# One more matrix product of 64 columns ahead of each step of a gated two-layer network (Trainium2, one core)

## The chip, the cores and the metric

The kernel runs on one core of one Trainium2 chip. The metric is the device time of one execution in microseconds (us); of several executions the median is taken. Each kernel also has one execution that the hardware profiler recorded, with its own time and its span (first to last instruction).

## The reference

Attention with a capped score for 4 x 12 heads of 448 tokens and 64 features, then two matrix layers over all 1792 tokens with a gate between them.

```python
scores = cap * np.tanh((scale * np.matmul(q, k.transpose(0, 1, 3, 2))) / cap)
scores = scores - np.max(scores, axis=-1, keepdims=True)
attn = np.exp(scores)
attn = attn / (np.sum(attn, axis=-1, keepdims=True) + 1e-09)
out = np.matmul(attn, v)            # (4, 12, 448, 64)
x = out.transpose(0, 2, 1, 3).reshape(4 * 448, 768)
h = x @ w_in                        # w_in: 768 x 2048
g = h * np.cos(h)
return g @ w_out                    # w_out: 2048 x 768
```

## The kernel before, in words

The first part is attention. A table of due times sets the order of its pieces; its products are of type float32. It leaves x, transposed, as two tiles `xh` and `xl` (a high part rounded to the type float32r, and the rest), each 128 partitions x 6 chunks of features x 1792 tokens.

The second part is the two layers. The 2048 hidden features are 16 blocks of 128, taken in 8 groups of two (`GF` = 2), and the 1792 tokens are 4 batches of 448 (`S`). A step is one group with one batch, so there are 32 steps. In each, two `Unit`s (j = 0 and 1, one for each hidden block) compute the first layer's product with `hidden`: 6 chunks times 3 terms (high x high, low x high, high x low) are 18 matmuls of a 128 x 128 weight tile with 448 columns, summed in one PSUM bank. A bank holds 512 columns of float32, so its columns 448 to 511 stay unused. Then the `Block` of the step before computes the second layer's product: three calls, each of 24 / 2 = 12 matmuls for two output chunks. So PE gets 36 matmuls of the first layer (L196) and 36 of the second (L601) in a step, 72 in all, all float32r with 448 columns.

Units use the pool tag `single`, which has two banks, so that unit 0 of a step gets the bank that unit 0 of the step before had. The second layer's sums go to the tags `pair` and `rest`. Behind the product of a unit, ScalarE and VectorE compute the gate from the bank: `turns` (L558), `whole_turns`, `reduce` (L566, L567), `cosine` (L570), `gate` (L573, the last reader of the bank), `high` (L576) and `low` (L579). VectorE also adds the second layer's sums into `acc` (L613) and turns the weights, which arrive as 64-bit words, into float32r pairs (L246 to L256).

`terms` changes the order of the three terms from group to group: even groups begin with the high part of x, odd groups with the low part; both begin with the high part of the weights (`wh`).

The first step's units are computed earlier, inside the last stretch of attention: `begin(0)` and `begin(1)` put their products into banks of the tag `pair`.

Of the kernel before, what the change touches and what calls it, by code (L numbers as in the profile page):

```python
# [19 lines left out]
B, H, S, D = 4, 12, 448, 64  # L20
# [149 lines left out]
class Banks:  # L170
# [14 lines left out]
    def product(self, i):  # L185

        return self.rest() if i == 2 else self.pair()


def hidden(nc, wts, f, xh, xl, h, b):  # L190
    hi, lo = wts.get("wi", f)
    toks = slice(S * b, S * b + S)
    for k in range(KC):
        ks = slice(128 * k, 128 * k + 128)
        for i, (w, x) in enumerate(terms(f // GF, hi, lo, xh, xl)):
            nc.tensor.matmul(h[:, 0:S], lhsT=w[:, ks], rhs=x[:, k, toks],  # L196
                             start=(k == 0 and i == 0), stop=(k == KC - 1 and i == 2))


def terms(G, wh, wl, xh, xl):  # L200

    if G % 2:
        return (wh, xl), (wh, xh), (wl, xh)
    return (wh, xh), (wl, xh), (wh, xl)
# [334 lines left out]
class Unit:  # L539
# [6 lines left out]
    def product(self, bank=None):  # L546
        if self.h is None:
            h = bank if bank is not None else self.m.banks.single()
            hidden(self.m.nc, self.m.wts, self.f, self.m.xh, self.m.xl, h, self.b)
            self.h = h[:, 0:S]  # L550

# [218 lines left out]
```

## Time and profile before

| what | value |
|---|---|
| median of 3 runs | 664.13 us (663.76 to 664.15) |
| profiled execution, its time | 664.33 us |
| profiled execution, its span | 662.5 us |
| mean granted TensorE clock | 0.994 of full |
| PE (matmuls) busy | 651.9 us, 98% |
| PEld (weight loads) busy | 490.0 us, 74% |
| DVE (VectorE) busy | 493.8 us, 75% |
| ACT (ScalarE) busy | 318.1 us, 48% |

The busy time of an engine is the time in which at least one of its instructions was under way. Matmuls overlap in the records, so the busy time of PE is not a sum of their durations; the distance from start to start tells their pace. The time of the profiled execution is 1.8 us more than its span.

### The profile page before, as it was taken

Reading aid. Unit: us, or ns where it says so; the run is one execution under the profiler, and the core shown is the slowest. Engines: PE = TensorE matmul, PEld = TensorE weight load, DVE = VectorE, ACT = ScalarE, POOL = GpSimd, SP = SyncE. Lnnn points to the kernel's source line nnn. Section 1 sums busy time; section 2 is a strip of 40 time slices with the busy share of each in tenths; the row PEclk is TensorE's granted clock in tenths of the full one; section 3 lists DMA queues with packets and bytes.
Section 4 is the critical chain, followed back from the end, with each engine's and each line's share of the span. In section 5 each row is a group of like instructions: output and inputs, shape, how many; then the busy total and the mean of one; then the engine's idle time right before and its main releaser. Section 6 shows DMA issues by size and latency. Waiting matters only on the chain.

```text
span 662.5 us, 8791 instructions
## 1 busy us (share of the span) xinstructions
PE 651.9 (98%) x3563; PEld 490.0 (74%) x3563; DVE 493.8 (75%) x739; ACT 318.1 (48%) x385; POOL 62.0 (9%) x39
## 2 busy tenths in 40 slices
PE   7999999999999999999999999999999999999996
PEld 2333333333489999999999999999999999999995
DVE  1599999997778876677777776677777776677663
ACT  4999999999724433333333333333333333333220
POOL 0001011000011111111111111111111121111000
PEclk9899999999999999999999999999999999999998
DMA  7044332542001211111112111111112111110224
GB/s 257 10 151 147 111 139 92 182 150 102 1 1 50 94 49 47 48 47 48 48 52 85 55 47 48 48 48 49 48 57 72 63 48 48 48 48 0 84 85 171
DMA packets 19616, 49.41 MB, mean 75 GB/s; under 512 B 2160, under 2 KB 5232, under 8 KB 19568
## 3 DMA queue, kind: packets, MB, share of 16 engines
q1 hardware_dynamic: 19568, 48.77, 21.8%
q8 instruction: 30, 0.49, 0.3%
q14 instruction: 18, 0.15, 0.1%
HBM read 43.25 MB, written 5.51 MB: 74 GB/s over the span
## 4 chain that ended last, share of the span: by engine, by line
PE 98%; ACT 1%; DMA 0%; issue 0%; DVE 0%
PE single L196 35%; PE pair L601 24%; PE rest L601 12%; PE single L421 12%; PE pair L328 9%; PE rest L337 3%; PE rest L430 2%; PE pair L196 1%; DMA capt<-in_cap_dram 0%; PE rest L102 0%; ACT t L362 0%; ACT late L347 0%; ACT t L347 0%; DVE acc L613 0%; ACT cabs L126 0%
## 5 line engine op out<-in xcount | busy, mean ns | idle before, releaser
L570 ACT ACTIVATE y<-y,angles 128x448 f32<-128x448 f32 x64 | 43.0, 672 | 149.4 <-DVE y L567 149.4
L558 ACT ACTIVATE v<-single,angles 128x448 f32<-128x448 f32 x62 | 39.2, 633 | 101.4 <-PE single L196 101.4
L246 DVE TENSOR_SCALAR u<-u 128x768 f32<-128x768 f32 x28 | 15.7, 561 | 94.9 <-ACT u L231 94.9
L613 DVE TENSOR_TENSOR acc<-pair,acc 128x896 f32<-128x896 f32 x56 | 60.6, 1083 | 3.9 <-PE pair L601 3.9
L576 ACT CAST gh<-y 128x448 fp32r<-128x448 f32 x64 | 36.3, 567 | 49.6 <-DVE y L573 49.6
L328 PE MATMUL pair<-qk 64*128 64x448 f32 x264 | 58.6, 562 | 0.0
L328 PEld LDWEIGHTS pair<-qk 64*128 64x128 f32 x264 | 22.7, 186 | 36.2 <-issue 20.1
L347 ACT ACTIVATE t<-pair,inv 128x896 f32<-128x896 f32 x48 | 45.9, 1004 | 6.0 <-PE pair L328 5.5
L579 DVE TENSOR_TENSOR gl<-y,gh 128x448 fp32r<-128x448 f32 x64 | 40.8, 638 | 4.0 <-ACT gh L576 4.0
L362 ACT ACTIVATE t<-t,capt 128x1792 f32<-128x1792 f32 x24 | 42.8, 1783 | 0.4
L401 DVE TENSOR_TENSOR sum<-t 128x896 f32<-128x896 f32 x24 | 26.1, 1088 | 21.9 <-ACT t L362 21.9
L567 DVE SCALAR_TENSOR_TENSOR y<-v,y 128x448 f32<-128x448 f32 x64 | 40.0, 625 | 2.2
L421 PE MATMUL single<-late,v 128*32 128x448 f32 x368 | 40.7, 542 | 0.0
L573 DVE TENSOR_TENSOR y<-single,y 128x448 f32<-128x448 f32 x62 | 38.2, 616 | 2.7 <-ACT y L570 2.7
L566 DVE SCALAR_TENSOR_TENSOR y<-v,single 128x448 f32<-128x448 f32 x62 | 38.5, 621 | 2.1
L421 PE MATMUL single<-t,v 128*32 128x448 f32 x368 | 39.4, 547 | 0.0
L601 PE MATMUL pair<-gh,wo0h 128*128 128x448 f32 x96 | 35.3, 368 | 0.0
L601 PE MATMUL pair<-gh,wo0l 128*128 128x448 f32 x96 | 35.3, 368 | 0.0
L601 PE MATMUL pair<-gl,wo0h 128*128 128x448 f32 x96 | 35.3, 368 | 0.0
L196 PE MATMUL single<-xl,wi2h 128*128 128x448 f32 x96 | 35.3, 368 | 0.0
L196 PE MATMUL single<-xh,wi2h 128*128 128x448 f32 x96 | 35.3, 368 | 0.0
L196 PE MATMUL single<-xh,wi2l 128*128 128x448 f32 x96 | 35.3, 368 | 0.0
(143 smaller groups left out, 1609.5 us busy)
## 6 DMA issues: line engine op xcount, KB each, us to landing
w<-in_w_in_dram SPq DMA_DIRECT2D x32, 384.0 KB, 3.6
w<-in_w_out_dram SPq DMA_DIRECT2D x32, 384.0 KB, 3.6
qk<-in_qkv_dram SPq DMA_DIRECT2D x22, 480.0 KB, 5.5
v<-in_qkv_dram SPq DMA_DIRECT2D x23, 256.0 KB, 4.0
out_dram<-acc SPq DMA_DIRECT2D x11, 448.0 KB, 2.5
w<-in_qkv_dram SPq DMA_DIRECT2D x2, 240.0 KB, 3.8
second<-in_qkv_dram SPq DMA_DIRECT2D x1, 480.0 KB, 5.7
out_dram<-acc SPq DMA_DIRECT2D x2, 224.0 KB, 2.8
```

The lines of the kernel that those rows point to most:

```text
L196: nc.tensor.matmul(h[:, 0:S], lhsT=w[:, ks], rhs=x[:, k, toks], start=(k == 0 and i == 0), stop=(k == KC - 1 and i == 2))
L328: self.nc.tensor.matmul(ps[:, h, 0:S], lhsT=x[mine, 128 * g:128 * g + 128], rhs=x[mine, Q], start=True, stop=True)
L347: self.nc.scalar.activation(out, ps[:, :, 0:S], AF.Tanh, scale=self.inv)
L362: self.nc.scalar.activation(t, t, AF.Exp, scale=self.capt)
L421: self.nc.tensor.matmul(self.acc[q][e][o], lhsT=self.v[q, a][:, g, d], rhs=t, start=(g == first), stop=(g == last), tile_position=(0, o.st ...
L558: m.nc.scalar.activation(self.v, self.h, AF.Identity, bias=m.quarter, scale=1.0 / (2.0 * math.pi))
L566: m.nc.vector.scalar_tensor_tensor(self.y, self.v, -TWO_PI_HI, self.h, op0=ALU.mult, op1=ALU.add)
L567: m.nc.vector.scalar_tensor_tensor(self.y, self.v, -TWO_PI_LO, self.y, op0=ALU.mult, op1=ALU.add)
L570: self.m.nc.scalar.activation(self.y, self.y, AF.Sin, bias=self.m.half_pi)
L579: self.m.nc.vector.tensor_sub(self.g[1][:, self.j], self.y, self.g[0][:, self.j])
L601: m.nc.tensor.matmul(y[:, e, 0:S], lhsT=w[:, c], rhs=x[:, j], start=(j == 0 and k == 0), stop=(j == GF - 1 and k == 2))
L613: m.nc.vector.tensor_add(acc, y[:, e, 0:S], acc)
```

## The change

Before the product of unit 0 of each step, one more matmul is issued. It multiplies the weight tile of chunk 0 (high part) with the first 64 tokens of chunk 0 of `xh`, and writes 64 columns into columns 448 to 511 of the unit's bank. Nothing reads them. It happens once in each of the 32 steps, the first of them in `begin(0)`.

```diff
     def product(self, bank=None):
         if self.h is None:
             h = bank if bank is not None else self.m.banks.single()
+            if self.j == 0:
+                hi, x = self.m.wts.get("wi", self.f)[0], self.m.xh
+                self.m.nc.tensor.matmul(h[:, S:512], lhsT=hi[:, 0:128], rhs=x[:, 0, 0:512 - S], start=True, stop=True)
             hidden(self.m.nc, self.m.wts, self.f, self.m.xh, self.m.xl, h, self.b)
             self.h = h[:, 0:S]
```

PE's instructions before, where one step of the layers ends and the next begins (`rest` is the bank of the last sum of the second layer, `single` the bank of unit 0; `wi0h` and `wi0l` are the high and low part of a weight tile; the semaphores that an instruction waits for stand in brackets):

```order
L601 MATMUL rest<-gh,wo1h 128x448
L601 MATMUL rest<-gh,wo1l 128x448
L601 MATMUL rest<-gl,wo1h 128x448
L196 MATMUL single<-xh,wi0h 128x448 [waits DVE_49]
L196 MATMUL single<-xh,wi0l 128x448
L196 MATMUL single<-xl,wi0h 128x448
```

The same place of PE in the changed kernel (three lines further down in the source, so L601 is L604 there):

```order
L604 MATMUL rest<-gh,wo1h 128x448
L604 MATMUL rest<-gh,wo1l 128x448
L604 MATMUL rest<-gl,wo1h 128x448
L551 MATMUL single<-xh,wi0h 128x64 [waits DVE_49,PE_49]
L196 MATMUL single<-xh,wi0h 128x448
L196 MATMUL single<-xh,wi0l 128x448
L196 MATMUL single<-xl,wi0h 128x448
```

The new matmul takes over the wait for VectorE, and a wait for PE's own semaphore is added: the columns 448 to 511 of this bank were last written by the new matmul of the step before, and its end is what is waited for, 73 matmuls back. For the second wait a separate waiting instruction stands ahead of the new matmul in 30 of the 32 steps (not shown above). The kernel before has 23 such waiting instructions in its layers, one of them ahead of the second layer's first matmul of the step that begins at 217 us. On the other engines the order is the same as before.

The beginning of the first unit, inside attention, before (PE; `t_1342` is a tile of exponentials, `pair` the bank of the unit):

```order
L421 MATMUL single<-t_1302,v 32x448 x2
L421 MATMUL single<-t_1342,v 32x448 x2
L196 MATMUL pair<-xh,wi0h 128x448 [waits Activation_49]
L196 MATMUL pair<-xh,wi0l 128x448 [waits Pool_49]
L196 MATMUL pair<-xl,wi0h 128x448
```

The same place in the changed kernel:

```order
L421 MATMUL single<-t_1302,v 32x448 x2
L421 MATMUL single<-t_1342,v 32x448 x2
L551 MATMUL pair<-xh,wi0h 128x64 [waits Activation_49]
L196 MATMUL pair<-xh,wi0h 128x448
L196 MATMUL pair<-xh,wi0l 128x448 [waits Pool_49]
L196 MATMUL pair<-xl,wi0h 128x448
```

Here too the new matmul takes over the wait of the first one of the unit, and nothing else moves.

## Rows read from the trace of the kernel before

**Rows 1.** The page: span, and the ended-last chain's shares by engine and line.

```profile
span 662.5 us, 8791 instructions
...
PE 98%; ACT 1%; DMA 0%; issue 0%; DVE 0%
PE single L196 35%; PE pair L601 24%; PE rest L601 12%; PE single L421 12%; PE pair L328 9%; PE rest L337 3%; PE rest L430 2%; PE pair L196 1%; DMA capt<-in_cap_dram 0%; PE rest L102 0%; ACT t L362 0%; ACT late L347 0%; ACT t L347 0%; DVE acc L613 0%; ACT cabs L126 0%
```

**Rows 2.** The chain in order of time, 379.89 to 412 us: start, length, what.

```profile
380.71 7.44 PE single L196 x36
388.15 4.96 PE pair L601 x24
393.12 2.48 PE rest L601 x12
395.60 7.44 PE single L196 x36
```

**Rows 3.** All waits of PE in the execution: total us, times, longest us.

```profile
PE pair L328 <- ACT t L347: 2.0, 1, 2.0
PE idle L102 <- DVE busy L112: 1.2, 1, 1.2
PE rest L102 <- ACT cabs L126: 1.0, 1, 1.0
```

**Rows 4.** Stretches: length, each engine's busy us (instructions), granted clock, DMA.

```profile
175.00:187.20 12.20, 12.20 (x85) 8.07 (x78) 10.21 (x17) 4.35 (x6) 0.00 (x0) 1.00 0.00 0
395.60:410.48 14.88, 14.88 (x73) 13.51 (x73) 11.09 (x19) 5.18 (x9) 1.85 (x1) 1.00 0.18 54
187.20:648.00 460.80, 460.80 (x2232) 418.48 (x2231) 340.64 (x521) 158.59 (x247) 53.55 (x29) 1.00 0.16 54
```

**Rows 5.** PE's timeline where a step ends and the next begins: start, length.

```profile
409.90 0.37 PE L601 MATMUL rest<-gh,wo1h 128*128 128x448 f32 x1
410.11 0.37 PE L601 MATMUL rest<-gh,wo1l 128*128 128x448 f32 x1
410.31 0.37 PE L196 MATMUL single<-xh,wi0h 128*128 128x448 f32 x1
410.52 0.37 PE L196 MATMUL single<-xh,wi0l 128*128 128x448 f32 x1
```

**Rows 6.** The weight loads of the same place.

```profile
410.11 0.19 PEld L196 LDWEIGHTS single<-xh,wi0h 128*128 128x128 f32 x1
410.32 0.19 PEld L196 LDWEIGHTS single<-xh,wi0l 128*128 128x128 f32 x1
```

**Rows 7.** Weight loads and matmuls of `begin(0)`, timelines of PEld and PE.

```profile
175.56 0.19 PEld L196 LDWEIGHTS pair<-xh,wi0h 128*128 128x128 f32 x1 [0.73 <-ACT late L347]
175.67 0.19 PEld L196 LDWEIGHTS pair<-xh,wi0l 128*128 128x128 f32 x1
175.87 0.19 PEld L196 LDWEIGHTS pair<-xl,wi0h 128*128 128x128 f32 x1
...
175.56 0.47 PE L196 MATMUL pair<-xh,wi0h 128*128 128x448 f32 x1
175.87 0.36 PE L196 MATMUL pair<-xh,wi0l 128*128 128x448 f32 x1
...
179.11 0.36 PE L196 MATMUL pair<-xl,wi0h 128*128 128x448 f32 x1
```

**Rows 8.** Weight loads of an odd group, two in a row of one tile.

```profile
400.19 0.19 PEld L196 LDWEIGHTS single<-xl,wi3h 128*128 128x128 f32 x1
400.40 0.19 PEld L196 LDWEIGHTS single<-xh,wi3h 128*128 128x128 f32 x1
400.60 0.19 PEld L196 LDWEIGHTS single<-xh,wi3l 128*128 128x128 f32 x1
```

**Rows 9.** VectorE's timeline: a unit's gate and the step's first own work.

```profile
404.36 0.62 DVE L573 TENSOR_TENSOR y<-single,y 128x448 f32<-128x448 f32 x1
...
410.97 1.08 DVE L613 TENSOR_TENSOR acc<-rest,acc 128x896 f32<-128x896 f32 x1
415.68 0.56 DVE L246 TENSOR_SCALAR u<-u 128x768 f32<-128x768 f32 x1 [3.63 <-ACT u L231]
```

**Rows 10.** PE's timeline at the change from the first layer to the second, one step.

```profile
224.11 0.37 PE L196 MATMUL single<-xl,wi1h 128*128 128x448 f32 x1
224.31 0.37 PE L601 MATMUL pair<-gh,wo0h 128*128 128x448 f32 x1
224.52 0.37 PE L601 MATMUL pair<-gh,wo0l 128*128 128x448 f32 x1
```

## The prediction

> **What bounds the kernel now.** I read the page first: the chain that ended last is 98% PE, and its largest parts are the two layers' matmuls, L196 and L601 [rows 1]. The chain in order of time then shows how the layers are laid out: 36 matmuls of the first layer in 7.44 us, 24 and 12 of the second in 4.96 and 2.48 us, and the next step begins at once [rows 2]. So a step is 14.88 us for 72 matmuls, 0.2067 us each, and the reader is to see that the chain never leaves PE there. The waits of PE say the same from the other side: in the whole execution it waited for another engine three times, 4.2 us together, all of them lines of attention or of the start (L102, L328) and none in the layers [rows 3]. The stretches give the other engines' share of one step: VectorE works 11.1 of 14.88 us, ScalarE 5.2, GpSimd 1.9, the DMA engines 18% [rows 4]. The granted clock is 1.00 through all the layers and in the stretch of the two early units, which is the 2.4 GHz level [rows 4]. Whatever PE does longer in a step therefore moves the end by as much, unless it fits into a gap of PE, and no such gap shows: the product that begins a step starts 0.20 us behind the last one of the step before [rows 5].
>
> **How a matmul and its weight load follow each other.** Each matmul has a weight load of its own. In the steady pace the load for a matmul starts as the matmul ahead of it starts, and not earlier: the load for the product of 410.31 starts at 410.11, the one for 410.52 at 410.32 [rows 5, 6]. So one weight tile is loaded ahead and no more. A record of a load is 0.19 us long, a pace is 0.21 us, and one could read from this that the load sets the pace. The beginning of the early units says that it doesn't. There the first load had nothing to hide behind: it starts at 175.56, and the second load starts at 175.67, 0.11 us later, while the second matmul starts at 175.87, 0.20 us behind that [rows 7]. Since a load starts as the matmul ahead starts, the first matmul began to stream at 175.67. So the weights are in place 0.11 us after the load begins, though its record is longer, and a matmul of 448 columns holds the array for some 0.20 us, behind which a load of 0.11 us is hidden.
>
> **The change, part by part.** It removes nothing. It adds 32 matmuls of 64 columns, 32 weight loads, 30 waiting instructions, and no work elsewhere.
>
> The new matmul's own load hides behind the last matmul of the step before, as the load at 410.11 does now [rows 6]: 0.11 us under 0.2067 us, nothing. If that cover were gone, it would cost its 0.11 us again.
>
> The new matmul itself streams 64 columns. No product of this width is in the trace. Scaled from 448 columns it is 64 / 448 x 0.2067 = 0.03 us; with what the pace of 0.2067 us holds beyond 448 columns at 2.4 GHz (0.187 us), 0.02 us, as a fixed part, it is 0.027 + 0.02 = 0.047 us.
>
> What comes behind it is the point. The load for the first real product can start only as the new matmul starts, and needs 0.11 us. The real product cannot begin before that, however short the new one is. Until now its load lay under a matmul of 0.2067 us; now it lies under one of 0.03 to 0.05 us and sticks out. So a step becomes longer by the load, 0.11 us, in which the 64 columns are hidden, and not by the columns. That the weights are the same tile doesn't help as far as the trace goes: in odd groups two matmuls in a row use the high part of one tile, and it is loaded twice, 0.21 and 0.20 us apart as everywhere [rows 8].
>
> The price has two ends. Below it is the columns alone, 0.03 us, if this one load could come earlier; above it is a full place in the pace, 0.207 us, if a load and its matmul could not follow each other faster than everywhere in the layers. I take 0.11 us, since the one place that shows a load without cover has it. If the 0.02 us came on top, it would be 0.13 us.
>
> On this the Trainium skill speaks, and against the load as the price: "TensorE: Matmul & The Clock Gate", section "Back-to-back issue gap", lists an isolated product of 1 to 64 columns at a floor of about 25 ns, or about 62 ns where the sequencer's microcode decodes it. By that table the sum would be an estimated 0.8 to 2.0 us. By the uncovered load of [rows 7] it is 3.5 us. The table leaves the weight load out, and I go by the row.
>
> The waiting instructions cost nothing, I say. VectorE's last read of a bank, its gate, starts at 404.36 and takes 0.62 us, and the bank is next written at 410.31, over 5 us later [rows 5, 9]. The wait for PE's own semaphore is for a matmul of a step ago, 14.9 us. That a separate waiting instruction on PE by itself costs no time is seen at 224.31, where the kernel before has one: the distances are 0.20 and 0.21 us, the common pace [rows 10]. The matmuls ahead are still streaming while PE takes in the wait; without that cover its price has, from these rows, no more than their rounding, 0.01 us, which is 0.3 us in 30 steps.
>
> The other engines get 0.11 us more in each step. VectorE, the busiest, waits in each step anyway: it ends its last addition of one step at 412.05 and starts the next weight work at 415.68 [rows 9]. Nothing of theirs becomes late. The one new matmul inside attention, at `begin(0)`, meets a PE that is busy throughout 175 to 187 us [rows 4], so it counts like the rest.
>
> The sum: 32 x 0.11 = 3.5 us. The profiled execution has 664.33 us, so 667.8 us by its own time; it lies 0.2 us above the median of the runs, so against 664.13 us the forecast is 667.6 us. That is 0.5%, and I call 0.2%, 1.3 us, about what a measurement here tells from no change.
>
> **The rivals.**
> The pace of the load: a load and a matmul together need 0.207 us, always. For it speaks that a load's record is 0.19 us and that loads stand 0.207 us apart throughout the layers [rows 6, 8]; against it that the second load of the early unit started 0.11 us behind the first [rows 7]. It gives 32 x 0.207 = 6.6 us, 670.7 us.
>
> The columns alone: the load comes early enough after all, or is left out for the same tile. Then 32 x 0.03 to 0.047 = 1.0 to 1.5 us, 665.1 to 665.6 us, at the edge of no change. Against it stand [rows 6, 8].
>
> No cost at all, since PE would have waited at a step's beginning: 664.1 us. Against it stand [rows 3, 5].
>
> Not slower, but faster: the pace is not a constant. In the first early unit, 16 distances from 175.87 to 179.11 are 3.24 us, 0.2025 us each [rows 7], against 0.2067 us in the layers [rows 2]. What makes the difference the trace doesn't show; that unit came behind an uncovered load. If a short product, with its uncovered load, brought the shorter pace back for the rest of the step, it would give 72 x 0.0042 = 0.30 us and cost 0.11 us: 0.19 us gained in each of 31 steps, 6 us, 658 us. It decides from 26 products per step at the shorter pace on (0.11 / 0.0042). Against it: the pieces of the chain have 0.2067 us per product throughout, also behind the begin of a step [rows 2].
>
> **How the numbers follow.** The uncovered load, at 0.10 to 0.13 us, has 72%: 667.3 to 668.3 us, with the scatter of the runs 667.0 to 668.7 us. The full place has 12% (670.7 us), the columns alone 7% (half of it under 0.2%), no cost 4%, the faster pace 5%. The range has to take in the full place to hold 8 in 10: 666.7 to 670.9 us, 84%. Slower by over 0.2%: 72 + 12 + 4 = 88%; within 0.2%: 7%; faster: 5%.
>
> **What would show it.** In the profile after, the load for the first real product of a step should start with the new matmul, and this product some 0.11 us behind it; a step should be 14.99 us instead of 14.88 us, with PE's waits unchanged, the granted clock in the layers still 1.00, and the distances between the other products still 0.2067 us. A real product 0.03 to 0.05 us behind the new one would prove the columns right, 0.2 us the full place. I am wrong as a whole if the distances of the 72 others change, or if PE waits at the new matmul.

## The result, and the profile after

The changed kernel takes 657.96 us (median of 4 runs, 656.83 to 658.62) against 664.14 us before (4 runs, 663.76 to 664.27): a ratio of 0.9906, 95% interval [0.9889, 0.9923]. It is faster by 6.2 us, where 667.6 us and a range of 666.7 to 670.9 us had been forecast. The rival that ends on the other side, a shorter pace of the other products, had been given 5% and 658 us.

The page after, its span and the granted clock in 40 slices, which answer to [rows 1] and to the clock of [rows 4]:

```profile
span 655.7 us, 8917 instructions
...
PEclk9999999999999999999999999999999999999999
```

PE still is 98% of the chain, and its waits are the three of [rows 3] to 0.1 us, so no wait went away. A step of the layers after, as a stretch (length, busy us of PE, PEld, DVE, ACT, POOL with instructions, granted clock, DMA), which answer to [rows 4]:

```profile
405.58:420.28 14.70, 14.70 (x74) 13.63 (x73) 11.08 (x18) 5.16 (x9) 1.85 (x1) 1.00 0.17 54
```

A step is 14.70 us, where it was 14.88 us with one product less, at the same granted clock of 1.00. PE's timeline at the begin of such a step, and at its end, which answers to [rows 5] (L604 is the second layer here, L551 the new product):

```profile
405.38 0.36 PE L604 MATMUL rest<-gh,wo1l 128*128 128x448 f32 x1
405.58 0.19 PE L551 MATMUL single<-xh,wi0h 128*128 128x64 f32 x1
405.61 0.45 PE L196 MATMUL single<-xh,wi0h 128*128 128x448 f32 x1
405.90 0.36 PE L196 MATMUL single<-xh,wi0l 128*128 128x448 f32 x1
...
420.08 0.36 PE L604 MATMUL rest<-gh,wo1l 128*128 128x448 f32 x1
420.28 0.19 PE L551 MATMUL single<-xh,wi0h 128*128 128x64 f32 x1
```

And the weight loads at its begin, which answer to [rows 6]:

```profile
405.38 0.19 PEld L551 LDWEIGHTS single<-xh,wi0h 128*128 128x128 f32 x1
405.59 0.19 PEld L196 LDWEIGHTS single<-xh,wi0h 128*128 128x128 f32 x1
405.69 0.19 PEld L196 LDWEIGHTS single<-xh,wi0l 128*128 128x128 f32 x1
405.90 0.19 PEld L196 LDWEIGHTS single<-xl,wi0h 128*128 128x128 f32 x1
```

Two things are to be seen. The first real product's load starts with the new product, at 405.59, and the load behind it at 405.69. Since a load starts as the matmul ahead starts, the real product starts 0.11 us behind the new one (405.58 to 405.69). That is the price that had been forecast. (The record of the real product starts at 405.61 already and is 0.45 us long where others have 0.36 us; it seems to take in the wait for its weights.) But from 405.90 to 420.08 there are 70 distances in 14.18 us, 0.2026 us each, where all were 0.2067 us before. This is the pace of the early unit in [rows 7], now in the layers from step 1 on. The two early units themselves, the first of them with the new product ahead of it, ran at 0.2067 us in this profile.

From the first real or new product of step 1 to the last product the profiles have 468.5 us before (187.11 to 655.63) and 462.8 us after (185.06 to 647.88), 5.7 us less. Worked out: 2268 products at 0.0040 us less are 9.1 us, 31 new products at 0.11 us are 3.4 us, together 5.7 us less. The rest of the 6.8 us between the two spans lies ahead of the layers and behind them. `begin(0)` starts at 175.56 us in the profile before and at 173.33 us after, and in the thirteen profiles of this study anywhere from 173.2 to 176.0 us, whatever the kernel. The kernel before itself took 661.4 to 664.7 us on the chips of the later runs. With such a scatter, a median that meets a forecast to 0.1 us, as some do below, does so in part by luck; the distances in the profiles are the better evidence.

### The profile page after: what moved, and what is told of

Read it like the earlier page. It is cut to its first block, busy times and chain, and to the rows that moved or that the text cites. A ratio compares the mean times of both kernels' runs of the same rounds, so it can differ in the third digit from the quotient of the medians.

```text
span 655.7 us, 8917 instructions
## 1 busy us (share of the span) xinstructions
PE 644.2 (98%) x3595; PEld 493.5 (75%) x3595; DVE 493.7 (75%) x739; ACT 317.9 (48%) x385; POOL 61.9 (9%) x39
## 4 chain that ended last, share of the span: by engine, by line
PE 98%; ACT 1%; DMA 0%; issue 0%; DVE 0%
PE single L196 35%; PE pair L604 24%; PE rest L604 12%; PE single L421 12%; PE pair L328 9%; PE rest L337 3%; PE rest L430 2%; PE pair L196 1%; DMA capt<-in_cap_dram 0%; ACT t L362 0%; PE rest L102 0%; ACT late L347 0%; PE single L551 0%; ACT t L347 0%; DVE acc L616 0%
## 5 line engine op out<-in xcount | busy, mean ns | idle before, releaser
L196 PE MATMUL single<-xl,wi3h 128*128 128x448 f32 x96 | 35.1, 366 | 0.0
L604 PE MATMUL pair<-gh,wo0l 128*128 128x448 f32 x96 | 35.1, 365 | 0.0
L604 PE MATMUL pair<-gh,wo0h 128*128 128x448 f32 x96 | 35.1, 365 | 0.0
L196 PE MATMUL single<-xh,wi3l 128*128 128x448 f32 x96 | 35.1, 365 | 0.0
```

Source lines behind the costliest of these rows:

```text
L604: m.nc.tensor.matmul(y[:, e, 0:S], lhsT=w[:, c], rhs=x[:, j], start=(j == 0 and k == 0), stop=(j == GF - 1 and k == 2))
```

## The experiments

The theory after the result: PE has two paces for these products, and keeps either until something disturbs the rhythm of load and product; the new product (called a push from here on) disturbs it, and the short pace comes of that. Rivals: that the push is needed in each step, that it is the waiting instructions, or that any added instruction does it.

**One push, ahead of step 1.**

```diff
-            if self.j == 0:
+            if (self.f, self.b) == (0, 1):
```

> The new product once, ahead of unit 0 of step 1, and nowhere else. Theory (the pace has two states, and the new product's uncovered load moves PE from 0.2067 to 0.2027 us per product, where it stays): 31 steps and the last block are 2268 products, each 0.004 us shorter, 9.1 us less for 0.1 us more: 655.2 us, with 0.2027 us from step 1 to the end. Rival A (each step needs its own push, the short pace dies out within a step): 0.2 us less at most, 663.9 us. Rival B (it is the 30 separate waiting instructions or the semaphore counts, none of which stands here): 664.2 us.

Ten runs with a median of 661.87 us, in two groups: three of 654.52 to 655.47 us (the short group), seven of 661.44 to 664.63 us (the long group, where the kernel before lay too, with 661.41 to 664.55 us). Neither the theory nor a rival had said that. The profiled execution was one of the short group; its chain in order of time (start, length, what):

```profile
187.18 7.37 PE single L196 x36
194.55 4.87 PE pair L604 x24
199.42 2.43 PE rest L604 x12
201.85 7.30 PE single L196 x36
209.15 4.86 PE pair L604 x24
```

From the push on all is short: 7.30 us for 36 products are 0.2028 us each, and it stays so to the end, 30 steps without another push. So A and B fall for this execution: one push is enough, with no waiting instruction ahead of it. What happened in the seven others was open.

**One push, ahead of the first early unit.** The same line with `(0, 0)`.

> The new product only ahead of the first early unit, inside attention. Theory: what counts is the state in which the layers begin, and the attention products behind the first early unit start it anew, so the layers run at 0.2067 us: 664.1 to 664.3 us. Rival (any one such product sets the short pace for good): 655 us.

655.30 us (653.43 to 656.14, 4 runs), ratio 0.9875 [0.9846, 0.9905]: the time of the rival. But its reason isn't the rival's. In the profile, which shows one of the four runs, the first early unit runs at the short pace and the second at the long one. So the layers begin at the long pace, and change in the middle of step 1, far from any push. PE's timeline there:

```profile
195.90 0.37 PE L604 MATMUL pair<-gh,wo1l 128*128 128x448 f32 x1
196.10 0.36 PE L604 MATMUL pair<-gl,wo1h 128*128 128x448 f32 x1
196.30 0.36 PE L604 MATMUL pair<-gh,wo0h 128*128 128x448 f32 x1
196.50 0.36 PE L604 MATMUL pair<-gh,wo0l 128*128 128x448 f32 x1
196.69 0.37 PE L604 MATMUL pair<-gl,wo0h 128*128 128x448 f32 x1
```

And the weight loads, with VectorE's work ahead of them:

```profile
195.28 0.62 DVE L582 TENSOR_TENSOR gl<-y,gh 128x448 fp32r<-128x448 f32 x1 [0.63 <-ACT gh L579]
195.95 0.19 PEld L604 LDWEIGHTS pair<-gl,wo1h 128*128 128x128 f32 x1
196.10 0.19 PEld L604 LDWEIGHTS pair<-gh,wo0h 128*128 128x128 f32 x1
```

The load for `gl,wo1h` starts at 195.95, 0.05 us behind the start of the matmul ahead (195.90) and not with it: it is the one that waits for VectorE's `low` of the first step, which ends at 195.90. Its product is on time all the same, at 196.10. Behind it the distances are short, 0.20 us and 0.19 us in the rows, 0.2027 us on average to the end. So here the pace changed at a load that started late, with no added product near it. And the same place can explain the seven runs above: what sets the pace anew in step 1 may also undo the push ahead of it.

**A push that covers its load: 448 columns.** In each step; the first real product starts the columns over.

```diff
-                ...matmul(h[:, S:512], lhsT=hi[:, 0:128], rhs=x[:, 0, 0:512 - S], start=True, stop=True)
+                ...matmul(h[:, 0:S], lhsT=hi[:, 0:128], rhs=x[:, 0, 0:S], start=True, stop=True)
```

> In each step the added product has 448 columns instead of 64; it goes into the columns that the first real product then starts over. Theory: the load behind it is covered, so no state changes; each costs one place of the pace: 664.1 + 32 x 0.2067 = 670.7 us, at 0.2067 us throughout. Rival (any added instruction at the step's begin shifts the order of things enough): 664.1 - 9.3 + 32 x 0.2027 = 661.3 us.

670.82 us (668.51 to 671.27, 4 runs), ratio 1.012 [1.0095, 1.0144], as the theory said. Its chain:

```profile
396.35 0.21 PE single L551
396.56 7.44 PE single L196 x36
404.00 4.96 PE pair L604 x24
```

An added instruction by itself does nothing to the pace of the layers. (This kernel has no more separate waiting instructions than the kernel before, so it says nothing on those.) Each costs its place of 0.21 us. That is the price that the rival of the full place had named for 64 columns.

**One push, ahead of step 16.** The same line with `(8, 0)`.

> The new product once, ahead of unit 0 of step 16. Theory: 0.2067 us until there (410.3 us), 0.2027 us behind it: 16 steps and the last block are 1188 products, 4.75 us less for 0.1 us more, 659.5 us. Rival A (each step needs its own push): 664.0 us. Rival C (it is a matter of the first steps alone): 664.2 us.

659.40 us (657.61 to 659.90, 5 runs), ratio 0.9946 [0.9928, 0.9964], the theory's time. The chain around the push:

```profile
393.30 7.44 PE single L196 x36
400.74 4.96 PE pair L604 x24
...
408.21 7.37 PE single L196 x36
415.58 4.86 PE pair L604 x24
...
422.87 7.29 PE single L196 x36
```

By their times all five executions changed, none stayed at 664 us. The pace is long up to the push and short behind it (7.37 us with the 0.11 us of the load, then 7.29 us).

**Two pushes per step.** The condition `if self.j == 0:` becomes `if True:`.

> The new product of 64 columns ahead of both units of each step, 64 in all instead of 32. Theory (the short pace is a state; once in it, a further push only costs its load): 0.2027 us per product as with one per step, and 0.105 us more in each of 32 places, 3.4 us: 658.0 + 3.4 = 661.3 us. Rival (the pace gains with the number of pushes): below 658 us, with distances below 0.2027 us.

660.99 us (659.84 to 661.55, 4 runs), ratio 0.9954 [0.9937, 0.9972]: the theory's 661.3 us, and not below 658 us. This is the price of a push by itself. In the profiles the layers take 466.3 us here and 462.8 us in the changed kernel's second one (next paragraph), 3.5 us for 31 more pushes, 0.11 us each.

**The changed kernel again, and pushes ahead of steps 1 to 4 only.** The second with `(self.f, self.b) in ((0, 1), (0, 2), (0, 3), (2, 0))`.

> The changed kernel itself, on the same chip as the others of this call, for comparison: 658 us, with the short pace in the layers.

> The new product ahead of unit 0 of steps 1 to 4 alone. Theory, with pushes that take effect only sometimes, as the ten runs with one push of 654.5 to 664.6 us suggest: with four of them nearly all executions are in the short pace from step 4 on at the latest; 9.1 us less, 0.4 us more, up to 0.9 us lost where the first pushes fail: 655.4 to 656.3 us, some 2.5 us below the changed kernel. Rival (the short pace dies out in some executions and has to be set again and again): spread over 655 to 664 us as with one push.

658.79 us (656.70 to 659.35, 6 runs), ratio 0.9913 [0.9897, 0.9930], and 655.30 us (653.18 to 656.66, 4 runs), ratio 0.9862 [0.9839, 0.9885]: 3.5 us between them, where 27 pushes at 0.11 us are 3.0 us. The chain of the second, from step 1 on, shows what had been missing:

```profile
187.57 7.37 PE single L196 x36
194.94 4.93 PE pair L604 x24
199.87 2.48 PE rest L604 x12
...
202.38 7.37 PE single L196 x36
209.75 4.87 PE pair L604 x24
```

The push of step 1 gives 7.37 us. In the block behind it the pace falls back (4.93 us in part, then 2.48 us, the long value), at the same load for `gl,wo1h`, 0.03 us late here; and the push of step 2 brings the short pace back for good.

**Pushes of 224 columns.** In each step, `h[:, 0:224]` with `x[:, 0, 0:224]`, started over by the first real product.

> In each step the added product has 224 columns, so that it lasts about as long as a load needs (0.093 us at 2.4 GHz against 0.105 us); it goes into columns that the first real product starts over. Theory (any shift of a load against the running product sets the short pace): 0.2027 us per product and about 0.11 us for each added one, 658.2 us. Rival (the pace changes only behind a product much shorter than its load): 0.2067 us stays and 3.5 us are added, 667.6 us.

658.53 us (657.85 to 659.08, 4 runs), ratio 0.9918 [0.9901, 0.9935], the theory's time. In its profile too the short pace was lost in the block of step 1, where the load for `gl,wo1h` came 0.19 us late. At the push of step 2 the real product starts 0.10 us behind it and the pace changes, though the load can stick out by little: half a product is 0.10 us by the long pace, the load 0.11 us, so some 0.01 us by this estimate. PE's timeline there:

```profile
201.78 0.37 PE L604 MATMUL rest<-gl,wo1h 128*128 128x448 f32 x1
201.99 0.27 PE L551 MATMUL single<-xh,wi0h 128*128 128x224 f32 x1
202.09 0.37 PE L196 MATMUL single<-xh,wi0h 128*128 128x448 f32 x1
202.30 0.36 PE L196 MATMUL single<-xh,wi0l 128*128 128x448 f32 x1
202.49 0.36 PE L196 MATMUL single<-xl,wi0h 128*128 128x448 f32 x1
```

**One push, ahead of step 2,** where no late load comes behind it: the line with `(0, 2)`. **No push, one product in two halves,** from the kernel before:

```diff
-            nc.tensor.matmul(h[:, 0:S], lhsT=w[:, ks], rhs=x[:, k, toks],
-                             start=(k == 0 and i == 0), stop=(k == KC - 1 and i == 2))
+            parts = (0, 224, S) if (f, b, k, i) == (0, 2, 0, 1) else (0, S)
+            for c, d in zip(parts, parts[1:]):
+                nc.tensor.matmul(h[:, c:d], lhsT=w[:, ks], rhs=x[:, k, S * b + c:S * b + d],
+                                 start=(k == 0 and i == 0), stop=(k == KC - 1 and i == 2))
```

And once more one push ahead of step 1.

> One new product of 64 columns, ahead of unit 0 of step 2. Theory (what sets the pace anew is any load that starts late against the running product; step 1 has one of its own, where the second layer's load waits for VectorE's gl, and it can undo a push made before it; from step 2 on there is none): every execution is at 0.2027 us from step 2 to the end, 30 x 72 + 36 = 2196 products, 8.8 us less and 0.1 us more, 655.4 us, with no execution above 657.5 us. Rival (one push takes effect by chance, whatever comes behind it): some executions above 661 us again, as with one push ahead of step 1.

> The kernel before, with no added product: in step 2 alone, unit 0's second matmul is made in two halves of 224 columns. Theory (it is the place of the load, not the product that nothing reads, nor waits that come with it): the load behind the first half starts in its usual place but the product behind it waits some 0.01 us for it, which was enough with the added products of 224 columns; 0.2027 us from there on, 655.3 us. Rival (an added write, its waits or its load of 0.08 us without cover are needed): 0.2067 us throughout, 664.1 us.

> One push ahead of step 1 again, for one more profile. Theory: a time near 655 us with 0.2027 us to the end, or one of 661 us and more, and then the distances go back to 0.2067 us at the first block of step 1, where the load of gl is late. Rival (the push itself fails): 0.2067 us directly behind the push.

The push ahead of step 2: 654.36 us (653.26 to 655.39, 4 runs), ratio 0.9856 [0.9831, 0.9881], all four in the short pace by their times; the rival's executions above 661 us didn't come. The halves: 654.65 us (653.38 to 655.85, 4 runs), ratio 0.9872 [0.9847, 0.9896]. The chain of the second around step 2 (L198 is the first layer here, L603 the second; 37 products in step 2):

```profile
185.08 7.44 PE single L198 x36
192.52 4.96 PE pair L603 x24
...
199.96 7.31 PE single L198 x37
207.27 4.86 PE pair L603 x24
```

One product cut in two, with the same columns, brings the short pace for the rest of the kernel. (The kernel has one separate waiting instruction more than the kernel before; it stands at 211.04 us, where the pace has long changed.) So neither the columns that nothing reads nor the waits that came with them are needed.

The third, a single run, had 664.85 us, the time of the long group. PE's weight loads in the first block of step 1, and the matmul ahead of the first of them:

```profile
195.79 0.37 PE L604 MATMUL pair<-gh,wo1l 128*128 128x448 f32 x1
195.84 0.19 PEld L604 LDWEIGHTS pair<-gl,wo1h 128*128 128x128 f32 x1
196.00 0.19 PEld L604 LDWEIGHTS pair<-gh,wo0h 128*128 128x128 f32 x1
```

And its chain there:

```profile
187.78 7.37 PE single L196 x36
195.14 4.93 PE pair L604 x24
...
202.56 7.44 PE single L196 x36
```

The push took effect (7.37 us) and was lost in the block, where the load for `gl,wo1h` starts at 195.84, 0.05 us behind the start of the matmul ahead, at 195.79. From there on all is long. The rival, that the push itself fails, is out for this execution. That the seven of the long group went the same way is likely by their times, but none of them has a profile.

## Why the prediction was wrong

The step that failed is the one that stood in the sum without being written as a term: that the distances of the 72 other products stay at 0.2067 us. They fell to 0.2027 us, 9.1 us over the layers, and outweighed the 3.4 us that were added. The text had the case as a rival, and with its price (0.30 us against 0.11 us per step, 658 us), and had set its chance at 5% by an argument that was none: that the pieces of the chain have 0.2067 us throughout, behind the begin of a step too [rows 2]. No begin of a step before had a disturbed load, so those pieces said nothing on what one does. Two places in the layers' kind of products had one, the two early units. The first, of [rows 7], had the other pace. The second, `begin(1)`, whose distances the prediction doesn't give, began with an uncovered load as well, and went on at the long pace (weight loads, then PE, before):

```profile
183.29 0.19 PEld L196 LDWEIGHTS pair<-xh,wi1h 128*128 128x128 f32 x1 [0.73 <-PE single L421]
183.40 0.19 PEld L196 LDWEIGHTS pair<-xh,wi1l 128*128 128x128 f32 x1
...
183.61 0.36 PE L196 MATMUL pair<-xh,wi1l 128*128 128x448 f32 x1
...
186.91 0.37 PE L196 MATMUL pair<-xl,wi1h 128*128 128x448 f32 x1
```

Those 16 distances are 3.30 us, 0.206 us each, where the first unit's are 3.24 us. So the trace before had one sighting for the rival and one against it, and 5% was too little for that.

That 657.96 us meets the rival's 658 us is partly luck. The rival let the short pace last for the rest of a step. The runs show that, where no late load undoes it, it lasts to the end of the kernel, so that the pushes in the later steps only cost (655.30 us with four, 658.79 us with all).

The other points, by their order:
- PE bounds the layers, and what PE does longer or shorter moves the end: right, the waits are the same and the sum of the layers comes out to 0.1 us.
- The new product's own load is hidden: right (405.38 to 405.58, a usual place).
- The next load sticks out and costs 0.11 us, with the 64 columns inside it: right, 0.11 us at 405.58 to 405.69, and 0.11 us from the two pushes per step. The table of the Trainium skill ("TensorE: Matmul & The Clock Gate", section "Back-to-back issue gap") would have had 25 to 62 ns; the measurement decides for the load.
- The full place as the price of 64 columns: out, only a covered product of 448 columns pays it.
- The waiting instructions cost nothing: right as far as seen. The changed kernel has them in 30 steps, and its steps are 72 x 0.2026 + 0.11 us, with nothing left for them.
- No change of the granted clock: right, 1.00 in the layers at both paces.

What sets the pace is shown to this extent. Both paces last over hundreds of products. The pace changed where a load and a product were shifted against each other: at a load that stuck out behind a short product, at a load that waited 0.05 us for VectorE, at a product cut in two. Inside the layers, every push of 64 or 224 columns that came upon the long pace in a profile, at steps 1, 2 and 16, brought the short one, and so did the cut. Behind the products of attention it was not so. Of four profiles with a push of 64 columns ahead of the first early unit, three had the long pace in that unit and one the short one; with no push, its uncovered load led to the short pace in four profiles and to the long one in three. Late loads went either way too. The load for `gl,wo1h` in step 1, coming late, turned the long pace into the short one once (0.05 us late), left the short pace as it was four times (0.03 to 0.12 us late) and turned it into the long one three times (0.03, 0.05 and 0.19 us late). So no length of the delay separates the two ends. What in PE makes two paces of the same instructions, and what decides at such a load, stays open.

## What to carry to other kernels

Before a pace of a bound engine is multiplied by a count, look in the trace whether the same form of instruction has another distance anywhere, and what stood ahead of it there: a state that lasts outweighs a cost that is paid once per step. Where one long row of equal products on PE sets the time, try one disturbance (one product in two halves) behind the last place where a load waits for another engine, and look at the distances; here this one cut is worth 1.3%, and 32 pushes are worth 0.9%. And give a rival a chance by the places in the trace that meet its condition (here two early units, one for it and one against it), and not by the many places that lack it.

## What the runs showed of the hardware that had not been expected

Float32r products of 448 columns with a full weight tile run at 0.2067 us or at 0.2027 us each at one granted clock of 1.00, and stay at one of them for over 2000 products. A kernel with one push early took 655.5 us in one profiled execution and 664.9 us in another, with the same instructions, by which of the two it was left in. A load that starts 0.05 us late doesn't delay its product (195.95 to 196.10), so at the long pace the 0.2 us between a load and its product are not what the load needs.
